# A gated linear-attention kernel: the chunk states computed by an add-then-multiply scan that reads PSUM

## The chip, the cores and the metric

The kernel runs on one core of one Trainium2 chip. The metric is device microseconds of one execution, as the median of several runs. The profile comes from one execution of its own.

## The reference

Three layers follow each other on a batch of 4 sequences of 768 tokens. The first is a gated linear attention with 8 heads of width 48, and it is the one that the change touches:

```
for t in range(S):
    state = alpha[:, :, t, :, None] * state + einsum('bhd,bhe->bhde', k[:, :, t], v[:, :, t])
    y[:, :, t] = einsum('bhd,bhde->bhe', q[:, :, t], state)
```

The second layer mixes each token with the one before it (`mu * x + (1 - mu) * x_prev`, once for keys, once for a gate), then computes `sigmoid(xr @ w_r) * (relu(xk @ w_k)**2 @ w_v)` with widths 384, 1024, 384. The third layer adds a rank-32 product along the sequence (`U`, `V`) and then a two-layer MLP of width 1536 (`w_ch1`, `w_ch2`), and adds its input.

## The kernel before

**Blocks.** The tokens are cut into 8 blocks of 384 (two halves for each of 4 sequences). `moe1(n)` is the second layer of block n, `moe2(n)` the third. All eight `moe1` come first, then all eight `moe2`. Their matrix products are done as three fp32r products of high and low parts (`mm3`), 128x128 by 384 columns each.

**Attention.** `attention(u)` works on a unit: four heads of one block, as two pairs of heads (`ph`, a pair lies on partitions 0:48 and 64:112). There are two units for each block, 16 in all, 8 of them in the first half of a sequence (`half` 0) and 8 in the second (`half` 1), which starts from a state carried over. A block is cut into 3 chunks of 128 tokens. For each pair `prep` forms decay products inside a chunk with two scans on VectorE (`G` backwards, `Fp` forwards; between them a maximum with the least decay on GpSimd, `aC`, and a reciprocal, `bt`) and scales keys and queries. `keys_by_token` transposes the scaled keys of each chunk on TensorE into a PSUM bank (`kk_b`) and ScalarE copies them to `KI`. `scores` forms the masked products within a chunk. `states` multiplies keys and values of each chunk into the same bank `kk_b` (`plan.S48` products), ScalarE copies that to `KV`, a scan over the chunks on VectorE (multiply by the decay `FX`, then add) gives the states at the ends of the chunks (`R`), and two VectorE products with the next chunk's decay give the states at the starts of the chunks (`ST`). In the second half of a sequence four ScalarE products and two VectorE adds first bring in the carried state. `outputs` adds the products of scores with values and of states with queries in two banks, and ScalarE copies them to `Xs`. The fourth pair's 96 rows are then moved by six small DMAs (`spread`) to the rows that the other three leave free.

**Start.** The attention of block 0 comes first (`first_attention`), unit 1, then unit 0. Its query, key and decay loads (`load_qka`) go to three tiles `T`; the pair `ph` 1 reuses the tile of pair 2 and so can be loaded only when that pair has been scaled. Each load of a pair issues one DMA a head. Behind it the weights of `moe1` (`w_k`, `w_v`, `w_r`, stored in 64 bits) are loaded into raw buffers, decoded by ScalarE and VectorE, and split into a high and a low part. DMAs are all issued by SP, in order.

**Order.** The program's instructions are collected as work items with an engine, a cost and dependences. `Plan.schedule` is a list scheduler that puts them in an order for each engine: a first order by due times (`DUE`), then ten rounds by times from a backward pass; the order that ends first in its own model is issued. A PSUM bank counts as one item for dependences. While the planner sees TensorE idle it puts in small bf16 products of a zero tile (L395, `warm`), which write a part of a bank that nobody reads. Where both inputs of a VectorE operation are in SBUF, the planner keeps GpSimd's operations apart from it (`lock`).

**End.** `moe2` adds the last three row tiles to `u` on VectorE into `x2_ring`, a ring of two buffers, and a DMA takes each to the output.

## Time and profile before

| | |
|---|---|
| time, median of 3 runs | 724.15 us (722.25 to 725.62) |
| time of the profiled execution | 724.62 us |
| its span, from the first to the last instruction | 722.9 us |
| TensorE matmul busy | 705.5 us (98%) |
| VectorE busy | 508.5 us (70%) |
| ScalarE busy | 354.5 us (49%) |
| GpSimd busy | 75.8 us (10%) |

The profiled execution took 1.7 us more than its span. TensorE's busy time counts the small products of zeros too. Times within the execution count from the start of the span.

### The profile page before, as it was taken

The numbers are of one execution on the slowest core, as the hardware profiler recorded it, in microseconds if no ns is written. First come the engines' busy times: TensorE is split into PE (matmuls) and PEld (weight loads), VectorE is DVE, ScalarE is ACT, GpSimd is POOL, SyncE is SP. The second block draws the span as 40 slices with busy tenths as digits, with TensorE's granted clock in tenths as the row PEclk, the third lists the DMA queues.
The fourth block names the chain that finished last, engine by engine and source line by source line (L and its number), as shares of the span: only waits on it lengthen the run. The fifth ranks groups of instructions, "written<-read, shape, count | busy, mean of one in ns | idle before, by whom it ended". The sixth has DMA issues, their size and how long they took to land.

```text
span 722.9 us, 13907 instructions
## 1 busy us (share of the span) xinstructions
PE 705.5 (98%) x5319; PEld 675.4 (93%) x5319; DVE 508.5 (70%) x1173; ACT 354.5 (49%) x901; POOL 75.8 (10%) x131
## 2 busy tenths in 40 slices
PE   7999999999999999999999999999999999999995
PEld 7798889899999999999999999999999999999995
DVE  6898987897776567773699999575665657474611
ACT  2588656976767557677797672212121112111210
POOL 2021101442130311311002100000000000000000
PEclk9999989999999999999999999999999999999998
DMA  8835733434333222313253240102020202020001
GB/s 222 200 102 157 186 84 102 108 94 109 85 98 75 63 62 60 98 51 99 65 153 110 66 143 16 51 0 66 1 67 1 65 1 67 1 66 2 34 1 37
DMA packets 29484, 55.46 MB, mean 77 GB/s; under 512 B 5344, under 2 KB 20064, under 8 KB 29408
## 3 DMA queue, kind: packets, MB, share of 16 engines
q1 hardware_dynamic: 29408, 54.48, 27.3%
q8 instruction: 43, 0.70, 0.4%
q14 instruction: 33, 0.27, 0.1%
HBM read 43.85 MB, written 9.44 MB: 74 GB/s over the span
## 4 chain that ended last, share of the span: by engine, by line
PE 74%; DVE 6%; ACT 4%; DMA 3%; issue 1%; SPq 1%; DVEq 0%; ACTq 0%
PE bank L305 73%; DMA arena<-in_qka_dram 3%; ACT arena L320 2%; DVE arena L137 2%; DVE arena L982 2%; DVE rounded L137 1%; PE bank L310 1%; SPq L366 1%; ACT rounded L320 1%; DVE shared L137 1%; ACT shared L320 1%; DMA out_dram<-arena 0%; ACT bank L320 0%; DVE shared L349 0%; DVEq L137 0%
## 5 line engine op out<-in xcount | busy, mean ns | idle before, releaser
L305 PE MATMUL bank<-rounded 128*128 128x384 f32 x2232 | 424.3, 339 | 2.9 <-ACT rounded L320 1.2
L305 PEld LDWEIGHTS bank<-rounded 128*128 128x128 f32 x2232 | 383.7, 186 | 13.2 <-ACT arena L320 2.2
L305 PE MATMUL bank<-rounded,shared 128*128 128x384 f32 x864 | 164.9, 335 | 0.8 <-DVE rounded L137 0.5
L320 ACT ACTIVATE rounded<-bank 128x384 fp32r<-128x384 f32 x160 | 78.3, 489 | 175.4 <-PE bank L305 174.3
L305 PEld LDWEIGHTS bank<-rounded,shared 128*128 128x128 f32 x864 | 150.9, 188 | 1.7 <-DVE rounded L137 1.0
L320 ACT ACTIVATE arena<-arena 128x384 f32<-128x384 f32 (+6 forms) x234 | 103.2, 463 | 48.2 <-DMA arena<-in_qka_dram 29.4
L137 DVE SCALAR_TENSOR_TENSOR rounded<-bank,rounded 128x384 fp32r<-128x384 f32 x96 | 53.4, 556 | 91.4 <-ACT rounded L320 90.3
L982 DVE STREAM_TRANSPOSE arena<-arena 32x96 f32<-32x96 f32 x384 | 103.8, 270 | 5.7
L305 PE MATMUL bank<-shared 128*48 128x128 f32 (+3 forms) x1472 | 100.3, 266 | 3.4 <-DMA shared<-in_v_dram 1.2
L305 PEld LDWEIGHTS bank<-shared 128*48 128x48 f32 (+2 forms) x1472 | 86.6, 142 | 17.8 <-issue 6.2
L320 ACT ACTIVATE rounded<-arena 128x384 fp32r<-128x384 f32 (+2 forms) x137 | 70.4, 522 | 63.6 <-DVE arena L982 49.4
L137 DVE SCALAR_TENSOR_TENSOR arena<-arena 128x384 int32<-128x384 int32 (+2 forms) x140 | 79.9, 590 | 8.9 <-ACT arena L320 8.3
L320 ACT ACTIVATE bank<-bank 128x384 f32<-128x384 f32 x128 | 61.6, 482 | 23.4 <-PE bank L305 22.7
L137 DVE TENSOR_TENSOR rounded<-arena,rounded 128x384 fp32r<-128x384 f32 (+1 forms) x108 | 60.5, 570 | 11.4 <-ACT rounded L320 10.9
L137 DVE TENSOR_TENSOR arena<-bank,arena 128x384 f32<-128x384 f32 (+1 forms) x76 | 41.5, 552 | 25.0 <-PE bank L305 9.9
L137 DVE TENSOR_TENSOR rounded<-bank,rounded 128x384 fp32r<-128x384 f32 x64 | 35.4, 552 | 30.6 <-ACT rounded L320 28.9
L320 ACT ACTIVATE arena<-bank 112x384 f32<-112x384 f32 (+3 forms) x76 | 37.3, 504 | 35.2 <-PE bank L305 33.3
L137 DVE TENSOR_TENSOR shared<-bank,arena 128x384 f32<-128x384 f32 x64 | 33.9, 547 | 24.5 <-PE bank L305 23.0
L137 POOL TENSOR_TENSOR rounded<-arena,rounded 128x384 fp32r<-128x384 f32 (+1 forms) x25 | 27.7, 1116 | 110.5 <-ACT rounded L320 110.4
L395 PE MATMUL bank<-warm 128*128 128x128 bf16 x581 | 37.4, 224 | 1.1 <-DVE arena L543 1.1
L395 PEld LDWEIGHTS <-warm 128*128 128x128 bf16 x581 | 34.5, 101 | 3.1 <-issue 1.5
L349 DVE TENSOR_TENSOR_SCAN shared<-arena 128x384 f32<-128x384 f32 x32 | 31.0, 967 | 4.4 <-ACT arena L320 4.3
(47 smaller groups left out, 258.3 us busy)
## 6 DMA issues: line engine op xcount, KB each, us to landing
arena<-in_qka_dram SPq DMA_DIRECT2D x56, 216.0 KB, 3.7
arena<-in_w_dram SPq DMA_DIRECT2D x24, 384.0 KB, 3.5
shared<-in_v_dram SPq DMA_DIRECT2D x32, 144.0 KB, 3.0
x2d<-arena SPq DMA_DIRECT2D x24, 192.0 KB, 2.2
arena<-x2d SPq DMA_DIRECT2D x8, 576.0 KB, 4.1
out_dram<-arena SPq DMA_DIRECT2D x24, 192.0 KB, 1.9
arena<-in_w_v_dram SPq DMA_DIRECT2D x8, 384.0 KB, 3.2
arena<-in_qka_dram SPq DMA_DIRECT2D x24, 72.0 KB, 2.0
```

What stands on the lines that cost most here:

```text
L137: fn(**args)
L305: "PE", cost, [out], [lhsT, rhs], lambda out, lhsT, rhs: fn(out, lhsT=lhsT, rhs=rhs, start=start, stop=stop),
L310: self.add("PE", cost, [out], [in_, ident], lambda: self.nc.tensor.transpose(out, in_, ident))
L320: self.add("ACT", cost, outs, [in_] + extra, lambda out, in_: fn(out, in_, func, **kw), out=out, in_=in_)
L349: lambda: self.nc.vector.tensor_tensor_scan(out=out, data0=d0, data1=d1, initial=0.0, op0=ALU.mult, op1=ALU.add), True,
L366: lambda: self.nc.sync.dma_start(out, in_),
L395: lambda i: nc.tensor.matmul(banks[SPARE[i]][:, 384:512], lhsT=warm, rhs=warm, start=True, stop=True), FILL_UNTIL, ROUNDS
L982: plan.dve(284, [to], [src], lambda to=to, src=src: nc.vector.transpose(out=to, in_=src))
```

## The change

States: `KV` and the products after the scan go. The bank `kk_b` holds four columns for each head pair and element, and the scan reads it in PSUM: it adds a chunk's sum to the running value, then multiplies by the next chunk's decay, so that its result is already the state at the start of the next chunk. `fc` gets two more columns, a 1 for the first half (the fourth column then resets the scan by a factor 0). ScalarE copies the results to `ST`. In the second half of a sequence the carried state is copied into the bank's first column, and the last chunk's keys are no longer transposed or multiplied with the values, as no state after it is wanted.

Decay floor: the maximum with the least decay moves from GpSimd into the backward scan (`op1=max`, with the floor as the second input).

Start: a fourth tile for `T` lies on two of the raw buffers, so pair 1 has a tile of its own; the weights of `w_k` come in six loads rather than five. Odd heads load 48 rows rather than 64 at the start. The six small DMAs are issued after unit 1, and unit 0 copies its outputs for its two row ranges apart. The planner's cost for a DMA goes from 90 to 56 words a ns.

End: the last adds of `moe2` go into `rs`, three buffers. Operations of `prep` and `check_range` are restricted to partitions 0:112.

```diff
-    mix0_k=468, wk0=-238, wk1=-283, wk2=-17, wk3=45, wk4=60, wkk=7, wv=-12, r0=5, wr=37, early=31, x2=25, u=48, w1=227,
+    mix0_k=468, wk0=-238, wk1=-230, wk2=-220, wk3=38, wk4=45, wk5=60, wkk=7, wv=-12, r0=5, wr=37, early=31, x2=25, u=48, w1=227,
...
-    def scan(self, out, d0, d1):
+    def scan(self, out, d0, d1, op0=ALU.mult, op1=ALU.add):
         self.add(
             "DVE", 66.0 + 2.085 * out.free_size(), [out], [d0, d1],
             lambda: self.nc.vector.tensor_tensor_scan(
-                out=out, data0=d0, data1=d1, initial=0.0, op0=ALU.mult, op1=ALU.add
-            ), True,
+                out=out, data0=d0, data1=d1, initial=0.0, op0=op0, op1=op1
+            ), self.in_sbuf(d0, d1),
         )
...
-            "SP", max(cost, words / 90.0), [out if out_key is None else out_key], [in_ if in_key is None else in_key],
+            "SP", max(cost, words / 56.0), [out if out_key is None else out_key], [in_ if in_key is None else in_key],
...
+    T.append(view(arena, raw_at[2], (KD * TB + 1,)))
...
-    KV = new(2, D, NC)
-    carry = new(2, 2, D)
-    G, Fp, bt = (att(TB) for _ in range(3))
-    aC = new(NC)
+    carry = att(2, 2, D)
+    G, Fp = (att(TB) for _ in range(2))
...
-        nc.vector.memset(ends, 0.0)
+        nc.vector.memset(ends, DECAY_MIN)
...
+    def make_fc():
+
+        nc.gpsimd.memset(fc, 0.0)
+        nc.gpsimd.memset(fc.rearrange("p (b h n) c -> p b h n c", b=B, h=2)[:, :, 0, :, NC], 1.0)
+
+    plan.pool(200, [fc], [], make_fc)
...
-        return T[{2: 0, 3: 1, 0: 2, 1: 0}[ph] if ph < 4 else ph % 3]
+        return T[{2: 0, 3: 1, 0: 2, 1: 3}[ph] if ph < 4 else ph % 3]
...
+                n = D if hh else rows
                 plan.dma(
-                    t[64 * hh : 64 * hh + rows, a * TB : z * TB],
-                    bass.AP(src.tensor, src.offset, [[KD * TB, rows], [1, (z - a) * TB]]), in_key="in", cost=475.0,
+                    t[64 * hh : 64 * hh + n, a * TB : z * TB],
+                    bass.AP(src.tensor, src.offset, [[KD * TB, n], [1, (z - a) * TB]]), in_key="in", cost=475.0,
...
-        plan.act(first, ends[:, 0:NC], AF.Copy)
-        plan.scan(G[:, ::-1], at[:, 1 : TB + 1][:, ::-1], ends[:, ::-1])
-        plan.pool(160, [aC], [g0], lambda: nc.gpsimd.tensor_scalar_max(out=aC, in0=g0, scalar1=DECAY_MIN))
-        plan.dve(110, [bt], [aC], lambda: nc.vector.reciprocal(bt[:, 0:TB:CH], aC))
-        plan.pool(163, [f], [a0, g0], lambda: nc.gpsimd.tensor_tensor(out=f, in0=a0, in1=g0, op=ALU.mult))
+        plan.act(first, ends[BOTH, 0:NC], AF.Copy, scale=0.0)
+        plan.scan(g[:, ::-1], at[:, 1 : TB + 1][:, ::-1], ends[BOTH, ::-1], op1=ALU.max)
+        plan.dve(90, [bt], [g], lambda: nc.vector.reciprocal(bt[BOTH, 0:TB:CH], g[:, 0:TB:CH]))
+        plan.pool(163, [f], [a0, g], lambda: nc.gpsimd.tensor_tensor(out=f, in0=a0, in1=g[:, 0:TB:CH], op=ALU.mult))
         plan.at = due + 6
-        plan.scan(Fp, at[:, 0:TB], bt)
+        plan.scan(fp, at[:, 0:TB], bt[BOTH])
...
         plan.at = due
-        kt, kb = sub(kk_b, NC, 112), KB[ph % 2]
-        for c in range(NC):
+        m = NC - unit(ph // 2)[1]
+        kt, kb = sub(kk_b, m, 112), KB[ph % 2]
+        for c in range(m):
             plan.transpose(kt[:, c, :], kb[BOTH, c * CH : (c + 1) * CH], ident[BOTH, BOTH])
         for h, r in enumerate((EV, OD)):
-            plan.act(KI[ph % 2][:, h], kt[:, :, r], AF.Copy)
+            plan.act(KI[ph % 2][:, h, 0:m], kt[:, :, r], AF.Copy)
 
     def states(u, due):
+
+
 
         half = unit(u)[1]
         plan.at = due
-        kv, vs, st = sub(kk_b, 2, NC, D), VS[u % 2], ST[u % 2]
+        kv, vs, st = sub(kk_b, 2, D, NC + 1), VS[u % 2], ST[u % 2]
+        last = carry[BOTH, u % 2]
+        if half:
+            plan.act(kv[BOTH, :, :, 0], last, AF.Copy)
         for j in range(2):
-            for c in range(NC):
+            for c in range(NC - half):
                 for h, r in enumerate((EV, OD)):
-                    plan.mm(kv[r, j, c, :], KI[j][:, h, c, :], vs[:, h, c, j, :], True, True, plan.S48)
-        f = fc[BOTH, 2 * u : 2 * u + 2, :]
-        last = carry[BOTH, u % 2]
-        plan.act(
-            FX[BOTH, :, :, 1:], f[:, :, 1:].unsqueeze(2).to_broadcast([112, 2, D, NC - 1]), AF.Copy)
-        plan.act(KV[BOTH].rearrange("p j d c -> p j c d"), kv[BOTH], AF.Copy)
-        if half:
-            for j in range(2):
-                for h, r in enumerate((EV, OD)):
-                    plan.act(st[r, h, j, 0, :], carry[r, u % 2, j], AF.Copy, scale=fc[r, 2 * u + j, 0:1])
-            for h, r in enumerate((EV, OD)):
-                plan.tt(KV[r, :, :, 0], KV[r, :, :, 0], st[r, h, :, 0, :], ALU.add)
-        plan.scan(*(t[BOTH].rearrange("p j d c -> p (j d c)") for t in (R, FX, KV)))
+                    plan.mm(kv[r, j, :, half + c], KI[j][:, h, c, :], vs[:, h, c, j, :], True, True, plan.S48)
+        f = fc[BOTH, 2 * u : 2 * u + 2, 1 - half : NC + 2 - half]
+        plan.act(FX[BOTH], f.unsqueeze(2).to_broadcast([112, 2, D, NC + 1]), AF.Copy)
+        plan.scan(*(t[BOTH].rearrange("p j d c -> p (j d c)") for t in (R, kv, FX)), ALU.add, ALU.mult)
         for h, r in enumerate((EV, OD)):
-            plan.tt(
-                st[r, h, :, 1:, :], R[r, :, :, 0 : NC - 1].rearrange("p j d c -> p j c d"),
-                fc[r, 2 * u : 2 * u + 2, 1:].unsqueeze(3).to_broadcast([48, 2, NC - 1, D]), ALU.mult)
+            plan.act(
+                st[r, h, :, 1 - half :, :], R[r, :, :, 0 : NC - 1 + half].rearrange("p j d c -> p j c d"), AF.Copy)
         if not half:
             plan.act(last, R[BOTH, :, :, NC - 1], AF.Copy)
 
-    def outputs(u, due, spread):
+    def outputs(u, due, spread, apart=False):
...
-            plan.act(x[BOTH, p0 + j, 1:], two_b[j][BOTH, 0:TB], AF.Copy)
+            for r in (EV, OD) if apart else (BOTH,):
+                plan.act(x[r, p0 + j, 1:], two_b[j][r, 0:TB], AF.Copy)
...
-            outputs(u, due + 30, i == 1)
+            outputs(u, due + 30, i == 0, i == 1)
...
-            o = x2_ring()
+            o = rs[:, t, :]
...
-        ((P, raw_at[0]), (2 * P, raw_at[1]), (3 * P, rs_at), (P, raw_at[3]), (P, raw_at[0]))
+        ((P, raw_at[0]), (P, raw_at[1]), (3 * P, rs_at), (P, raw_at[2]), (P, raw_at[3]), (P, raw_at[0]))
     ):
-        raw = load_weight(w_k[:, :, c0 : c0 + n], at, -1650 if i < 4 else DUE["wk4"] - 60)
+        raw = load_weight(w_k[:, :, c0 : c0 + n], at, -1650 if i < 3 else DUE[f"wk{i}"] - 60)
```

## Rows read from the trace of the kernel before

**Rows 1.** Windows: stretch, length, busy (x) PE, PEld, DVE, ACT, POOL; clock, DMA, GB/s.
```profile
10.00:20.00 10.00, 7.95 (x119) 6.90 (x118) 6.44 (x11) 3.82 (x14) 0.79 (x3) 1.00 1.06 275
...
40.00:50.00 10.00, 9.43 (x153) 8.93 (x151) 9.30 (x21) 9.41 (x24) 2.18 (x1) 1.00 0.24 81
...
73.30:100.00 26.70, 25.79 (x266) 22.48 (x266) 24.46 (x49) 17.21 (x54) 2.40 (x8) 1.00 0.61 137
100.00:360.00 260.00, 258.85 (x2136) 240.68 (x2135) 184.66 (x349) 176.74 (x484) 54.66 (x86) 0.99 0.31 83
```

**Rows 2.** Windows, instructions of line L395 alone (the products of zeros).
```profile
0.00:73.30 73.30, 37.43 (x581) 34.50 (x581) 1.00 0.65 172
73.30:712.50 639.20, 0.00 (x0) 0.00 (x0) 0.99 0.24 66
```

**Rows 3.** Timeline of TensorE: start, us, operation, xcount, idle before and its releaser.
```profile
86.11 0.74 PE L305 MATMUL bank<-shared 128*48 128x48 f32 x24
86.78 0.44 PE L305 MATMUL bank<-rounded 128*128 128x384 f32 x1
...
88.81 0.51 PE L310 MATMUL bank<-arena,shared 112*128 112x112 f32 x3 [0.39 <-ACT arena L320]
```

**Rows 4.** The chain of work, in order of time: start, us, what.
```profile
154.10 0.29 PE bank L310 x3
```

**Rows 5.** Timeline of the end, TensorE, then VectorE, then SP.
```profile
714.95 0.69 PE L305 MATMUL bank<-shared,rounded 128*128 128x384 f32 x3
...
714.97 0.56 DVE L137 TENSOR_TENSOR arena<-bank,arena 128x384 f32<-128x384 f32 x1 [1.87 <-PE bank L305]
716.72 0.56 DVE L137 TENSOR_TENSOR arena<-bank,arena 128x384 f32<-128x384 f32 x1 [1.19 <-DMA out_dram<-arena]
```

**Rows 6.** Groups of instructions by form, whole span: busy us, mean ns | idle before.
```profile
L349 DVE TENSOR_TENSOR_SCAN shared<-arena,shared 128x384 f32<-128x384 f32 x32 | 31.7, 989 | 0.4
...
L349 DVE TENSOR_TENSOR_SCAN shared<-shared,arena 112x288 f32<-112x288 f32 x16 | 11.9, 747 | 1.1 <-ACT arena L320 1.1
...
L137 DVE TENSOR_TENSOR shared<-shared,arena 48x192 f32<-48x192 f32 x32 | 13.1, 409 | 0.4
...
L137 DVE TENSOR_TENSOR arena<-arena,shared 48x96 f32<-48x96 f32 x16 | 4.5, 279 | 0.3
...
L137 DVE TENSOR_TENSOR shared<-bank,arena 128x384 f32<-128x384 f32 x64 | 33.9, 547 | 24.5 <-PE bank L305 23.0 <-ACT arena L320 1.1
...
L137 DVE TENSOR_TENSOR shared<-arena,shared 128x384 f32<-128x384 f32 x44 | 23.9, 547 | 1.2 <-PE bank L305 0.7 <-DMA arena<-in_qka_dram 0.5
```

**Rows 7.** The same view, ScalarE and GpSimd.
```profile
L320 ACT ACTIVATE arena<-bank 112x288 f32<-112x288 f32 x16 | 9.0, 562 | 11.1 <-PE bank L305 10.7 <-PE bank L395 0.2
...
L320 ACT ACTIVATE shared<-arena 48x48 f32<-48x48 f32 x32 | 10.5, 328 | 0.3
...
L320 ACT ACTIVATE shared<-arena 112x192 f32<-112x192 f32 x16 | 5.7, 359 | 0.1
...
L320 ACT ACTIVATE arena<-shared 112x96 f32<-112x96 f32 x8 | 2.7, 332 | 5.9 <-DVE shared L349 5.7
...
L712 POOL TENSOR_SCALAR arena<-shared 128x3 f32<-128x3 f32 x32 | 12.7, 398 | 125.4 <-DVE shared L349 118.6 <-DVE shared L713 6.7
...
L320 ACT ACTIVATE arena<-bank 112x384 f32<-112x384 f32 x32 | 14.9, 489 | 12.3 <-PE bank L305 12.1
```

**Rows 8.** Timelines of the start: VectorE, then SP.
```profile
17.87 0.96 DVE L349 TENSOR_TENSOR_SCAN shared<-arena 128x384 f32<-128x384 f32 x1 [1.57 <-ACT arena L320]
...
36.72 0.56 DVE L137 TENSOR_TENSOR rounded<-arena,rounded 128x384 fp32r<-128x384 f32 x1 [1.47 <-ACT rounded L320]
...
9.25 1.11 SPq L366 DMA_DIRECT2D arena<-in_qka_dram  x2
...
32.38 0.52 SPq L366 DMA_DIRECT2D arena<-arena  x1
```

**Rows 9.** Windows of all instructions, a stretch at the low clock.
```profile
103.30:110.20 6.90, 6.90 (x48) 6.23 (x49) 4.71 (x9) 2.01 (x6) 0.38 (x2) 0.51 0.37 86
```

More of the change, by code (lines that the diff above doesn't have):

```diff
@@ L447, in fast_path @@
     low = new(NPH)
-    fc = new(NPH, NC)
+    fc = new(NPH, NC + 2)
     firsts = new(NPH, NC)
@@ L490, in fast_path @@
     VS = [att(2, NC, 2, D) for _ in range(2)]
-    FX, R = (att(2, D, NC) for _ in range(2))
+    FX, R = (att(2, D, NC + 1) for _ in range(2))
     ST = [att(2, 2, NC, D) for _ in range(2)]
-    KV = new(2, D, NC)
-    carry = new(2, 2, D)
-    G, Fp, bt = (att(TB) for _ in range(3))
-    aC = new(NC)
+    carry = att(2, 2, D)
+    G, Fp = (att(TB) for _ in range(2))
+    bt = new(TB)
     w1h, w1l = (view(shared, i * KD * DF2, (KD, DF2), F32R) for i in range(2))
@@ L554, in fast_path @@
     plan.dve(400, [bt], [], lambda: nc.vector.memset(bt, 0.0))
+    plan.pool(60, [low], [], lambda: nc.gpsimd.memset(low, 0.0))
+    def make_fc():
+        nc.gpsimd.memset(fc, 0.0)
+        nc.gpsimd.memset(fc.rearrange("p (b h n) c -> p b h n c", b=B, h=2)[:, :, 0, :, NC], 1.0)
+    plan.pool(200, [fc], [], make_fc)
     def make_tri():
@@ L567, in fast_path @@
         plan.pool(600, [t], [], lambda t=t: nc.gpsimd.memset(t, 0.0))
-    plan.pool(130, [FX[:, :, :, 0]], [], lambda: nc.gpsimd.memset(FX[:, :, :, 0], 0.0))
-    for t in banks[5:8]:
-        plan.dve(600, [t[32:64]], [], lambda t=t: nc.vector.memset(t[32:64], 0.0))
+    for t in (banks[5], banks[6][32:64], banks[7][32:64]):
+        plan.dve(600, [t], [], lambda t=t: nc.vector.memset(t, 0.0))
     def next_raw():
@@ L696, in check_pair @@
     def check_pair(ph, t):
-        there = junk[:, 0 : t.free_size()].rearrange("p (c t) -> p c t", c=t.shape[1])
-        plan.act(there, t, AF.Relu, scale=-1.0, bias=ALPHA_MIN, accum_out=low[:, ph : ph + 1])
+        there = junk[BOTH, 0 : t.free_size()].rearrange("p (c t) -> p c t", c=t.shape[1])
+        plan.act(there, t, AF.Relu, scale=-1.0, bias=ALPHA_MIN, accum_out=low[BOTH, ph : ph + 1])
     def prep(ph, due, engs):
-        qt, kt, at = q_k_a(tile_of(ph))
-        g0, f, a0 = G[:, 0:TB:CH], fc[:, ph, :], firsts[:, ph, :]
+        qt, kt, at = (t[BOTH] for t in q_k_a(tile_of(ph)))
+        g, fp, f, a0, first = G[BOTH], Fp[BOTH], fc[BOTH, ph, 0:NC], firsts[BOTH, ph, :], at[:, 0:TB:CH]
         if ph >= CHECK_LATER:
@@ L1029, in check_first @@
         plan.at = due
-        check_pair(ph, q_k_a(T[2])[2][:, 0:TB].unsqueeze(1))
+        check_pair(ph, q_k_a(T[2])[2][BOTH, 0:TB].unsqueeze(1))
     def check_range():
-        one = ck[:, 4:5]
+        c, one = ck[BOTH], ck[:, 4:5]
         for r, x in ((slice(0, P), 0.0), (EV, 1.0), (OD, 1.0)):
             plan.dve(70, [one[r]], [], lambda r=r, x=x: nc.vector.memset(one[r], x))
-        plan.dve(280, [ck[:, 5:6]], [firsts], lambda: nc.vector.tensor_reduce(
-            out=ck[:, 5:6], in_=firsts, axis=AX.XY, op=ALU.min))
-        plan.ts(ck[:, 5:6], ck[:, 5:6], ALPHA_MIN, None, op0=ALU.is_ge)
-        plan.dve(110, [ck[:, 0:1]], [low], lambda: nc.vector.tensor_reduce(
-            out=ck[:, 0:1], in_=low, axis=AX.X, op=ALU.max))
-        plan.dve(280, [ck[:, 1:2]], [fc], lambda: nc.vector.tensor_reduce(
-            out=ck[:, 1:2], in_=fc, axis=AX.XY, op=ALU.max))
-        plan.ts(ck[:, 2:3], ck[:, 0:1], 0.0, None, op0=ALU.is_le)
-        plan.ts(ck[:, 3:4], ck[:, 1:2], DECAY_MAX, None, op0=ALU.is_le)
-        plan.tt(ck[:, 2:3], ck[:, 2:3], ck[:, 3:4], ALU.mult)
-        plan.tt(ck[:, 2:3], ck[:, 2:3], ck[:, 5:6], ALU.mult)
+        plan.dve(280, [c[:, 5:6]], [firsts], lambda: nc.vector.tensor_reduce(
+            out=c[:, 5:6], in_=firsts[BOTH], axis=AX.XY, op=ALU.min))
+        plan.ts(c[:, 5:6], c[:, 5:6], ALPHA_MIN, None, op0=ALU.is_ge)
+        plan.dve(110, [c[:, 0:1]], [low], lambda: nc.vector.tensor_reduce(
+            out=c[:, 0:1], in_=low[BOTH], axis=AX.X, op=ALU.max))
+        plan.dve(280, [c[:, 1:2]], [fc], lambda: nc.vector.tensor_reduce(
+            out=c[:, 1:2], in_=fc[BOTH], axis=AX.XY, op=ALU.max))
+        plan.ts(c[:, 2:3], c[:, 0:1], 0.0, None, op0=ALU.is_le)
+        plan.ts(c[:, 3:4], c[:, 1:2], DECAY_MAX, None, op0=ALU.is_le)
+        plan.tt(c[:, 2:3], c[:, 2:3], c[:, 3:4], ALU.mult)
+        plan.tt(c[:, 2:3], c[:, 2:3], c[:, 5:6], ALU.mult)
         ps = kk_b[0:1, 0:1]
-        plan.mm(ps, ck[:, 2:3], one, True, True, 60.0)
+        plan.mm(ps, c[:, 2:3], one[BOTH], True, True, 60.0)
         plan.dve(70, ["ok"], [ps], lambda: nc.vector.tensor_copy(ok_i, ps))
```

5 lines of the change are left out of this document (2 added, 3 removed).

## The prediction

> **What bounds the kernel now.** I read the windows first, stage by stage, because a share over the whole span mixes two regimes. In the long middle TensorE never rests: busy 258.85 of 260 us between 100 and 360, while VectorE has 184.66 and ScalarE 176.74 [rows 1]. Whatever leaves TensorE's queue there shortens the run one for one, and whatever leaves VectorE or GpSimd is worth nothing there. The start is the other regime. TensorE looks busy too, but the windows of L395 alone say what with: 581 products of zeros, all before 73.3 us [rows 2]. Those are fillers that the planner puts where it sees TensorE without work, so before 73 us the limit is elsewhere. Between 40 and 50 us VectorE is at 9.30 and ScalarE at 9.41 of 10; between 10 and 20 the DMA engines are at 1.06 of their time with 275 GB/s [rows 1]. So the start is first a matter of loads, then of VectorE and ScalarE together, and TensorE can run full only once they have delivered. VectorE stays nearly full up to 100 us (24.46 of 26.7) with TensorE short of work for 26.7 - 25.79 = 0.91 us. The third place is the end: the last product ends at 714.95 + 0.69 = 715.64 us, but the last VectorE add starts only at 716.72, and its releaser is an output DMA [rows 5].
>
> **The middle: TensorE's work.** In the second half of a sequence (8 units, 16 pairs) a third of the transposes goes, 16 in all, and of the key-value products 2 pairs x 2 heads for each unit, 32 in all. A product is fp32 and shows as two instructions: the 12 of a unit stand as x24. They start at 86.11 and the next product starts at 86.78, so one instruction holds the queue for 0.67 / 24 = 28 ns [rows 3]. That is 64 x 28 = 1.79 us. Three transposes take 0.29 us on the chain, 97 ns each [rows 4], so 16 x 97 = 1.55 us. Sum: **3.34 us** less. Nothing hides this gain, because no filler is left after 73.3 us. The products that stay now write every fourth word of the bank; no row shows such a write. Below, it costs nothing; above, I allow a doubling, (192 - 32) x 2 x 28 ns = 9.0 us. I take nothing, because the key-value product's 28 ns are the shortest spacing in the rows and the address step changes no count of columns.
>
> **The middle: VectorE, ScalarE, GpSimd.** In the first half a unit loses a scan of 288 elements (747 ns) and two products (409 ns each) and gets a scan of 384 elements (989 ns): 1.565 to 0.989, 0.58 us less. In the second half two adds of 279 ns go as well: 2.123 to 0.989, 1.13 us less [rows 6]. The scan now reads PSUM. The nearest rows are VectorE products of one size with one input in PSUM or both in SBUF: 547 and 547 ns [rows 6], so I take no surcharge; with 0.1 us for each of the 16 scans VectorE would lose 1.6 of the 13.7 us that it gains. [...]
>
> ScalarE in the first half loses the copy to `KV` (562) and has a copy of 384 in place of 192 elements for `FX` and two copies to `ST` (192 elements each, like the 359 row). Copies of 96, 192 and 384 elements stand at 332, 359 and 489 ns, one of 288 at 562 with a rearranged output [rows 7]; so for 384 elements with a broadcast input I take 0.52, and 0.44 for 288. The sum is 0.36 + 0.56 + 0.33 = 1.25 before and 0.52 + 2 x 0.36 + 0.33 = 1.57 after, 0.32 us more. In the second half the four 328 ns products go: 2.23 before, 0.33 + 0.52 + 2 x 0.44 = 1.73 after, 0.50 us less [rows 7]. In the middle all of this is covered by TensorE, which has more to do than either engine; without that cover ScalarE would gain 8 x (0.50 - 0.32) = 1.4 us. GpSimd loses 32 maxima of 398 ns; it is busy for a tenth of the run, and the step only shortens the way between the two scans of `prep`. I cost it at nothing, as the scans wait in a full VectorE queue.
>
> **The start.** The four units of blocks 0 and 1 run before 100 us. Those of block 0 save 2 x 0.58 = 1.15 us of VectorE where VectorE is the limit; that counts in full. Those of block 1 save 2.27 us, but by then TensorE wants only 0.91 us more [rows 1], so I count 0.9. Pair 1 gets a tile: before, its loads were issued at 9.25 us, when pair 2 had freed its tile, and the scan on them began at 17.87 after VectorE had stood idle for 1.57 us [rows 8]. With its own tile the loads go out beside those of the other pairs, and I count the 1.57 us. The 48 rather than 64 rows take 4 x 16 x 4.6 KB = 0.29 MB from a full queue, 1.1 us at 275 GB/s [rows 1]; this makes the same loads land earlier, so I don't count it twice. The small DMAs: two of the six had to wait for unit 0's copies (the last kind is issued at 32.38), and VectorE then idles 1.47 us at 36.72 behind ScalarE's rounding of the mixed inputs [rows 8]. Now they wait for unit 1 alone; I count 1.47. Against this, ScalarE has 2 x 0.32 more for the states of block 0 and two more copies of 489 ns for unit 0's outputs [rows 7], 1.6 us, in a stage where it is as full as VectorE. Sum: 1.15 + 0.9 + 1.57 + 1.47 - 1.6 = **3.5 us** less. From below nothing, if ScalarE or the weights' loads set the pace; from above 1.15 + 2.27 + 1.57 + 1.47 + 1.1 = 7.6 us, if ScalarE has room. I take the sum, which is near the middle. The six loads of `w_k` rather than five, the new due times and the dearer DMA in the planner's eyes move work about in an order that is made anew; I give that no sign and 2 us in the range either way.
>
> **The end.** With a third buffer the last add follows the last product: 716.72 - 715.64 = **1.08 us** less [rows 5]. From below 0.5, if its DMA then shares the queue with the second. In the seven other blocks the same wait is behind TensorE's back.
>
> **Sum.** 724.62 - 3.34 - 3.5 - 1.08 = 716.7 us for an execution like the profiled one, which is 0.5 us above the median of 724.15.
>
> **Rivals.**
> *The start gives nothing* (ScalarE is as full as VectorE, 9.41 against 9.30 [rows 1]): 724.62 - 3.34 - 1.08 = 720.2 us. For it: the extra 1.6 us of copies. Against: VectorE's idle times are real and behind loads that now come earlier.
> [...]
> *The bank is held* (slower). Before, a copy of 562 ns on ScalarE freed the bank for the next transposes; now the scan on VectorE frees it, 989 ns after it has come to the head of a queue that is 92% full up to 100 us. Even before, transposes at 88.81 stood 0.39 us behind a ScalarE copy into the arena, where `KV` lies too, with every product behind them in TensorE's order [rows 3]. If each unit of blocks 0 and 1 waits 2 us there, 8 us are lost and the start's gain too: 720.2 + 8 = 728.2 us. It decides from 1.9 us a unit over these four, or 0.5 us over all 16. Against it: in the middle VectorE is 71% busy and TensorE has other products to put in between.
> *The order gives it back.* The gain is undone by more changes between long and short products or by DMAs that the dearer price puts later: about 4 us, 724 us, no change.
>
> **Chances.** Forecast (715 to 719 us) 0.50; the start gives nothing 0.15; the low clock goes or the start gives its upper bound 0.17; the order gives it back 0.10; the bank is held, or the write with a step is dear, 0.08. Faster by over 0.5% means under 720.5, slower over 727.8; half a per cent is about what a measurement of this kernel can tell from no change. Of the second case a little over half is under 720.5: 0.50 + 0.17 + 0.08 = 0.75 faster, 0.07 + 0.10 = 0.17 the same, 0.08 slower. The range goes from 711 (the start's upper bound, 712.6, less part of the low clock) to 721.5 (no gain at the start and a little lost to the order); about a tenth lies beyond each end.
>
> **What would show it.** Products on `kk_b`: 64 instructions and 16 transposes fewer, at 28 and 97 ns as before. Fillers that end before 70 us and number under 581. The scan on `kk_b` at about 0.99 us, and no wait of transposes behind it longer than 0.5 us. The first long product before 41 us. The last add within 0.1 us of the last product. I am wrong if the fillers end at 73 us again, if key-value products space out to 50 ns, or if TensorE's idle time after 100 us grows by more than 2 us.

## The result and the profile after

The changed kernel takes **703.92 us** (median of 4 runs, 702.96 to 705.15) against 723.21 us for the kernel before beside it (4 runs), a ratio of 0.973, 95% interval 0.970 to 0.976. The forecast was 716.7 us with a range from 711 to 721.5. The sign was right; the gain is 19.3 us where 7.9 was forecast, so the time lies below the range. The profiled execution took 704.0 us with a span of 702.3 us, 20.6 us shorter than before.

From the page of the changed kernel, busy time, the granted clock and the products of zeros (L395):

```profile
PE 692.5 (99%) x5188; PEld 664.9 (95%) x5188; DVE 491.2 (70%) x1125; ACT 360.2 (51%) x895; POOL 69.7 (10%) x102
...
PEclk9999999999999999999999999999999999999999
...
L395 PE MATMUL bank<-warm 128*128 128x128 bf16 x530 | 35.4, 229 | 1.1 <-DVE arena L543 1.1
```

The windows of the changed kernel, in the stretches of [rows 1], with the same columns:

```profile
10.00:20.00 10.00, 9.75 (x149) 8.49 (x149) 7.87 (x15) 4.14 (x14) 1.32 (x2) 1.00 0.76 179
...
40.00:50.00 10.00, 10.00 (x154) 9.84 (x152) 10.00 (x23) 7.66 (x22) 2.54 (x4) 1.00 0.72 208
...
73.30:100.00 26.70, 26.70 (x284) 22.64 (x278) 23.15 (x45) 18.58 (x55) 1.39 (x4) 1.00 0.57 127
100.00:360.00 260.00, 259.00 (x2078) 242.93 (x2077) 182.78 (x338) 194.27 (x509) 51.30 (x64) 1.00 0.34 91
```

The middle looks as before: TensorE 259.0 of 260 us. The start doesn't. Between 10 and 20 us VectorE does 7.87 us of work where it did 6.44, while the DMA engines move 179 GB/s where they moved 275; between 40 and 50 us they move 208 where it was 81, so transfers now come later. From 73.3 to 100 us TensorE lacks nothing any more. The stretch at a granted clock of 0.51 [rows 9] is gone: the mean granted clock of the profiled execution rose from 0.992 to 0.998.

Now the groups by form that answer to [rows 6, 7], busy us, mean ns and idle before. First three of TensorE in the kernel before, then the changed kernel:

```profile
L305 PE MATMUL bank<-shared 48*128 48x128 f32 x384 | 42.0, 291 | 0.9 <-DVE arena L648 0.9
...
L310 PE MATMUL bank<-arena,shared 112*128 112x112 f32 x96 | 15.6, 267 | 1.9 <-DVE shared L713 1.0 <-ACT shared L320 0.5 <-ACT arena L320 0.4
...
L305 PE MATMUL bank<-shared 128*48 128x48 f32 x384 | 14.6, 211 | 2.1 <-DMA shared<-in_v_dram 1.2 <-ACT shared L320 0.9
```

```profile
L305 PE MATMUL bank<-shared 48*128 48x128 f32 x384 | 40.2, 290 | 0.0
...
L310 PE MATMUL bank<-arena,shared 112*128 112x112 f32 x80 | 13.2, 262 | 0.1
L305 PE MATMUL bank<-shared 128*48 128x48 f32 x320 | 12.9, 212 | 0.2
...
L349 DVE TENSOR_TENSOR_SCAN shared<-arena 112x384 f32<-112x384 f32 x64 | 61.4, 972 | 3.7 <-ACT arena L320 1.9 <-POOL shared L137 1.2 <-issue 0.4
L349 DVE TENSOR_TENSOR_SCAN shared<-bank,shared 112x384 f32<-112x384 f32 x16 | 15.2, 948 | 0.3 <-PE bank L305 0.3
...
L320 ACT ACTIVATE shared<-shared 48x288 f32<-48x288 f32 x16 | 11.5, 721 | 4.4 <-DVE shared L349 4.2
L320 ACT ACTIVATE shared<-shared 48x192 f32<-48x192 f32 x16 | 8.7, 546 | 9.9 <-DVE shared L349 9.7
```

The key-value products are 320 where they were 384, at 212 ns a record where it was 211. Within a run of them one starts 25 ns after another on average (29 ns before), so no cost of writing every fourth word shows here. The transposes are 80 where they were 96, and TensorE waits 0.1 us before them in the whole run, so no wait shows that the bank is held. The scan that reads PSUM takes 948 ns, the same shape from SBUF 972 ns. It is 24 ns cheaper, so the 0.1 us for each of the 16 scans that the prediction sets against a source in PSUM are not there. The copies to `ST` are dear, 546 ns for 192 elements and 721 ns for 288.

The end, timelines of TensorE and of VectorE:

```profile
695.40 0.69 PE L305 MATMUL bank<-shared,rounded 128*128 128x384 f32 x3
...
696.13 0.56 DVE L137 TENSOR_TENSOR arena<-bank,arena 128x384 f32<-128x384 f32 x1 [0.31 <-PE bank L305]
```

The last product ends at 695.40 + 0.69 = 696.09 us and the last add starts 0.04 us later, released by TensorE and no longer by a DMA [rows 5].

**Where the 20.6 us are.** TensorE's records split the span into fillers (L395), idle time and all other work. Idle is the span less the busy time: 17.4 us before, 9.8 after, **7.6 us less**: 6.1 in the first 100 us, 0.4 from 100 to 690, the rest at the end. Fillers: 37.4 before [rows 2], 35.4 after, **2.1 less**. Other work: 668.1 before, 657.1 after, **11.0 less**. The busy times of groups overlap where their records do (those of the changed kernel add up to 770.5 us against 692.5 for TensorE), so they don't add up to this. Counted from the start of each record to the start of the next, less idle time, TensorE has 2.1 us less for the transposes, 2.1 for the key-value products, 1.9 for the products of `scores` (384 each time), 2.8 for the two groups of products in `outputs` and 2.2 for the long products. The low clock, by my estimate 6.9 x (1 - 0.51) = 3.4 us at most, is no term beside these: it lies in the records that ran between 103.3 and 110.2 us [rows 9]. Forecast were 3.5 for the start (idle and fillers there give 8.1), 3.3 for the removed work, 1.1 for the end and nothing for clock, scores and `outputs`.

### The profile page after: what moved, and what is told of

It is laid out like the page before. It is cut to its first block, busy times and chain, and to the rows that moved or that the text cites. A ratio compares the mean times of both kernels' runs of the same rounds, so it can differ in the third digit from the quotient of the medians.

```text
span 702.3 us, 13571 instructions
## 1 busy us (share of the span) xinstructions
PE 692.5 (99%) x5188; PEld 664.9 (95%) x5188; DVE 491.2 (70%) x1125; ACT 360.2 (51%) x895; POOL 69.7 (10%) x102
## 4 chain that ended last, share of the span: by engine, by line
PE 54%; DVE 8%; issue 1%; ACT 0%; DVEq 0%
PE bank L305 54%; DVE rounded L137 3%; DVE arena L987 2%; DVE arena L137 2%; DVE shared L349 1%; DVE shared L137 0%; PE bank L310 0%; ACT bank L320 0%; DVEq L137 0%; DVE arena L720 0%; DVEq L349 0%
## 5 line engine op out<-in xcount | busy, mean ns | idle before, releaser
L320 ACT ACTIVATE arena<-arena 128x384 f32<-128x384 f32 (+5 forms) x234 | 101.7, 462 | 23.0 <-DMA arena<-in_qka_dram 16.2
L320 ACT ACTIVATE rounded<-arena 128x384 fp32r<-128x384 f32 (+3 forms) x137 | 70.4, 523 | 68.0 <-DVE arena L987 48.1
L305 PEld LDWEIGHTS bank<-shared 128*48 128x48 f32 (+2 forms) x1408 | 80.3, 140 | 15.1 <-issue 7.9
L305 PE MATMUL bank<-shared 48*128 48x128 f32 (+3 forms) x1408 | 93.2, 264 | 0.4 <-ACT arena L320 0.2
L320 ACT ACTIVATE bank<-bank 128x384 f32<-128x384 f32 x128 | 61.1, 478 | 18.3 <-PE bank L305 17.4
L349 DVE TENSOR_TENSOR_SCAN shared<-arena 112x384 f32<-112x384 f32 x64 | 61.4, 972 | 3.7 <-ACT arena L320 1.9
L320 ACT ACTIVATE arena<-bank 112x384 f32<-112x384 f32 (+3 forms) x62 | 29.5, 487 | 22.3 <-PE bank L305 20.6
L395 PE MATMUL bank<-warm 128*128 128x128 bf16 x530 | 35.4, 229 | 1.1 <-DVE arena L543 1.1
L395 PEld LDWEIGHTS <-warm 128*128 128x128 bf16 x530 | 32.9, 103 | 2.5 <-DVE arena L543 1.1
```

What stands on the lines that cost most here:

```text
L305: "PE", cost, [out], [lhsT, rhs], lambda out, lhsT, rhs: fn(out, lhsT=lhsT, rhs=rhs, start=start, stop=stop),
L320: self.add("ACT", cost, outs, [in_] + extra, lambda out, in_: fn(out, in_, func, **kw), out=out, in_=in_)
L349: lambda: self.nc.vector.tensor_tensor_scan(out=out, data0=d0, data1=d1, initial=0.0, op0=op0, op1=op1), self.in_sbuf(d0, d1),
L395: lambda i: nc.tensor.matmul(banks[SPARE[i]][:, 384:512], lhsT=warm, rhs=warm, start=True, stop=True), FILL_UNTIL, ROUNDS
```

## The experiments

Orders are made anew by the planner for each kernel, so neighbours differ for no reason of their own: price 58 in place of 56 gives 702.03 us, 1.9 below the changed kernel. I read no single difference under 3 us as the work of an edit without a row for it. The kernel before has medians of 720.8 to 725.2 us beside these experiments; each ratio is to the runs of it that were taken beside that kernel. A useful sum for each kernel is TensorE's **lost time in the first 100 us**, idle plus fillers by the windows; before it is 100 - 92.30 + 37.43 = 45.1 us, after 100 - 98.36 + 35.36 = 37.0. It leaves out what an order loses behind 100 us; where that counts it is said.

### The DMA price alone, and the change without it

```diff
-            "SP", max(cost, words / 90.0), ...
+            "SP", max(cost, words / 56.0), ...
```

> The kernel before with the one edit that the planner prices a DMA at 56 words a ns. Theory A: fillers and idle time up to 75 us shrink by 4 to 7 us, VectorE's wait of 1.5 us at 22 us behind a weight load is gone, time 716 to 720 us. Theory B: 721 to 725 us, as pair 1 still waits for its tile and the mixing for the small DMAs.

> The changed kernel with one edit undone: the planner prices a DMA at 90 words a ns again. Theory A (the price is what shortened the start: with 90 the planner thinks loads land earlier than they do, puts the decoding of weights ahead of attention steps in the queues of VectorE and ScalarE, and both stand behind loads): TensorE's fillers and idle time up to 75 us grow by 4 to 7 us, the first long product moves from 31 us towards 37 or later, time 708 to 711 us. Theory B (the fourth tile and the early small DMAs shortened the start): no more than 2 us, 702 to 706 us, first long product at 31 to 33 us.

The kernel before with this one number changed: **713.39 us** (713.15 to 714.38), ratio 0.987 [0.984, 0.990]. The change with the old number: **715.5 us** (711.54 to 720.1), ratio 0.989 [0.982, 0.995]. Both lie outside what was expected of them, 713.4 below 716 to 720 and 715.5 above 708 to 711: the number that I gave no sign is worth 10 to 12 us, as much as all the rest.

Windows of the first 100 us, in turn of the kernel before, of the kernel before with price 56, of the changed kernel with price 90 (here also its two stretches at a granted clock of 0.50), and of the changed kernel:

```profile
0.00:100.00 100.00, 92.30 (x1151) 83.40 (x1152) 83.97 (x173) 63.35 (x175) 13.49 (x39) 1.00 0.64 163
```

```profile
0.00:100.00 100.00, 98.84 (x1219) 90.05 (x1220) 89.40 (x185) 66.77 (x182) 13.55 (x41) 1.00 0.61 167
```

```profile
0.00:100.00 100.00, 92.77 (x1089) 84.44 (x1089) 83.05 (x166) 67.68 (x178) 9.53 (x31) 0.97 0.63 164
...
15.10:18.50 3.40, 3.40 (x35) 3.18 (x34) 3.40 (x8) 3.13 (x9) 0.76 (x1) 0.50 1.08 368
...
97.00:107.30 10.30, 10.30 (x59) 8.96 (x61) 7.85 (x16) 3.36 (x10) 1.06 (x1) 0.50 0.26 68
```

```profile
0.00:100.00 100.00, 98.36 (x1187) 89.12 (x1187) 86.95 (x174) 70.35 (x188) 11.92 (x32) 1.00 0.67 171
```

With price 90 TensorE is idle for 7 to 8 us of the first 100 in either kernel, with 56 for 1.2 and 1.6. What it waited for at the start stands in the waits of the first 45 us (engine, line, waited for, us in all, times, longest). The kernel before:

```profile
ACT arena L320 <- DMA arena<-in_qka_dram: 11.1, 5, 3.6
DVE shared L349 <- ACT arena L320: 4.4, 4, 1.6
...
ACT arena L320 <- DMA arena<-in_w_k_dram: 2.6, 2, 2.3
```

and with price 56:

```profile
ACT arena L320 <- DMA arena<-in_qka_dram: 7.2, 5, 2.4
...
DVE shared L349 <- ACT arena L320: 1.9, 2, 1.2
```

At price 90 the planner believes that a load of 32-bit words runs at 360 GB/s. The DMA view of the kernel before, first 40 us in slices of 1 us, shows what was moved:

```profile
GB/s 0 0 131 146 303 195 249 230 263 232 223 360 221 218 176 307 354 386 331 179 181 271 301 372 136 25 48 48 251 194 157 333 215 154 136 283 198 316 109 9
DMA packets 4831, 8.24 MB, mean 206 GB/s; under 512 B 735, under 2 KB 3257, under 8 KB 4825
```

The mean of 206 is taken over stretches with loads and without: slices reach 386 GB/s and fall to 9, so it is not the rate of one load. As I read it, the planner at 90 puts ScalarE's and VectorE's work on a load into their queues ahead of its arrival, and work that is ready stands behind it. At 56 words a ns, 224 GB/s, it plans with nearly the mean that it gets, ScalarE's waits behind loads fall from 13.7 to 7.2 us, and no wait behind `w_k` is left. In the changed kernel the same waits are 11.6 us at price 90 and 8.3 at 56. That these waits carry the gain, and not some other difference of the orders, is argued from them and not shown apart.

The rest is clock. The runs of the changed kernel at price 90 took 711.54, 713.5, 717.5 and 720.1 us at mean granted clocks of 0.999, 0.995, 0.990 and 0.987: the two stretches above, 3.4 + 10.3 = 13.7 us at a granted clock of 0.50, are from the profiled execution, the one of 717.5. With no fall the old price still costs 711.5 - 703.9 = 7.6 us. Ahead of the second fall TensorE had waited 1.5 us behind ScalarE, up to 95.59 us. None of the four profiles of the changed kernel with a price from 45 to 72 has a fall before the end. Over all runs of the experiments the mean clock is under 0.995 in 37 of 55 at price 90, the kernel before among them, and in 3 of 64 (the changed kernel's own four included) at 45 to 58. So falls go with the price, but not strictly: the kernel before took 718.9 to 722.0 us in its nine runs at 0.997 or 0.998 and 725.0 to 727.0 in its ten at 0.987 to 0.989. Against the former, price 56 (713.39 us) is worth some 7 us. What in an order brings a fall on is not shown.

### Other prices

```diff
-            "SP", max(cost, words / 56.0), ...
+            "SP", max(cost, words / 58.0), ...   # and 45.0, 72.0
```

> A control: the changed kernel with the planner's price at 58 instead of 56 words a ns, which means nothing for the loads but makes another order. If the order made anew is a lottery of a few us, the time moves by 1 to 4 us either way; if the order is robust near a right price, 702.5 to 705.5 us.

> The changed kernel with the price at 45 words a ns, dearer than the loads are. If the right price is what counts, a slightly too dear one makes the planner wait a little but leaves no queue behind a load: 703 to 708 us. If dearer is always better: under 702 us.

> The changed kernel with the price at 72 words a ns, between 56 and 90. If the time follows how far the price is from what the loads do (206 GB/s in the first 40 us, 51 words of 4 bytes a ns): between 704 and 715.5 us, some 707 to 711 us. If only the particular order at 90 was unlucky: 700 to 706 us.

| price, words a ns | 45 | 56 | 58 | 72 | 90 |
|---|---|---|---|---|---|
| time, us | 706.28 | 703.92 | 702.03 | 708.48 | 715.5 |
| idle, first 100 us | 1.07 | 1.64 | 1.93 | 5.20 | 7.23 |
| idle, 100 to 690 us | 1.29 | 1.96 | 1.68 | 4.04 | 4.82 |

TensorE's idle time grows with a price that promises too fast a transfer, in the middle too, while its fillers in the first 100 us stay between 34.8 and 36.8 us (price 45 has 1.5 us more of them behind 100 us). From 45 to 58 the differences are those of neighbouring orders, so 56 is no sharp optimum.

### Start edits: on their own, and taken back one by one

On the kernel before at price 90: the fourth tile, six loads of `w_k` with the new due times and the small DMAs after unit 1. Then the changed kernel with the tile of pair 1 shared again, with the small DMAs late again, and with all start edits undone (48 rows too) but price 56 kept.

```diff
-        ((P, raw_at[0]), (P, raw_at[1]), (3 * P, rs_at), (P, raw_at[2]), (P, raw_at[3]), (P, raw_at[0]))
+        ((P, raw_at[0]), (2 * P, raw_at[1]), (3 * P, rs_at), (P, raw_at[3]), (P, raw_at[0]))   # new_old_start
...
-        return T[{2: 0, 3: 1, 0: 2, 1: 3}[ph] if ph < 4 else ph % 3]
+        return T[{2: 0, 3: 1, 0: 2, 1: 0}[ph] if ph < 4 else ph % 3]   # new_tile3
...
-            outputs(u, due + 30, i == 0, i == 1)
+            outputs(u, due + 30, i == 1)                                # new_spread_late
```

> The kernel before with the start's edits alone (fourth tile, w_k in six loads, early small DMAs) and the price still at 90. If the price is what counts: the queues still stand behind loads, 719 to 725 us. If the prediction's account of the start holds without the price: 2 to 4 us less, 719 to 721 us; and were the start's edits the cause of all that was not expected, 711 to 715 us.

> The changed kernel with pair 1 back in the tile of pair 2. Theory A (the price): at most 2 us, 703 to 706 us, as pair 1's decay landed only 0.9 us earlier with its own tile (16.46 instead of 17.34 us). Theory B (the tile): pair 1's loads go out some 2 us later again, unit 0 ends 2 to 4 us later, time 706 to 709 us.

> The changed kernel with the six small DMAs issued after unit 0 again, and its outputs copied in one piece. Theory A: under 2 us, 703 to 706 us. Theory B (they stood on the way from unit 0's outputs to the first long product, some 2.5 us from issue to landing): the first long product moves from 31 to 33 or 34 us and the time to 706 to 708 us.

> The changed kernel with all of the start's edits undone (pair 1 in pair 2's tile, small DMAs late, w_k in five loads at the old due times, 64 rows), price 56 kept. If the start's edits count for little at a right price: 700 to 705 us. If they are worth the 3.5 us of the prediction: 706 to 709 us.

Added alone: 724.02 us (10 runs), ratio 0.999 [0.997, 1.002]. Taken back: tile 703.07, ratio 0.972 [0.969, 0.975]; small DMAs 700.67, ratio 0.970 [0.966, 0.973], below what was expected either way; all of them 705.33, ratio 0.976 [0.971, 0.982], between the two expectations, with one of the four runs at 710.85 us and a mean clock of 0.990. The terms of 1.57 and 1.47 us of the forecast are not there in the times of either kernel. The lost time in the first 100 us with all undone is 100 - 98.22 + 35.65 = 37.4 us against 37.0, so the start edits together are worth 0.4 us there.

The small DMAs do what they were meant to do. TensorE's timeline of the changed kernel, then of the one with the small DMAs late:

```profile
30.99 0.62 PE L305 MATMUL bank<-rounded 128*128 128x384 f32 x2 [0.17 <-ACT rounded L320]
...
32.59 14.53 PE L395 MATMUL bank<-warm 128*128 128x128 bf16 x257
...
51.40 9.63 PE L305 MATMUL bank<-rounded 128*128 128x384 f32 x54 [0.15 <-ACT rounded L320]
```

```profile
35.53 0.60 PE L305 MATMUL bank<-rounded 128*128 128x384 f32 x2
...
51.02 9.63 PE L305 MATMUL bank<-rounded 128*128 128x384 f32 x54
```

The first long product comes 4.5 us earlier (in the kernel before it started at 41.01 us). But only 6 of them stand there: 14.5 us of fillers follow, and the long row of 54 starts at 51.40 us against 51.02. Between 40 and 50 us VectorE is busy all of the time (10.00 us), decoding and splitting weights for the most part; as I read it, that is what was late next. The 3.2 us by which late small DMAs are faster are of the size of another thing: the products of `scores` fill 36.9 us there rather than 40.2 (the last experiment says why).

### The states: the scan in PSUM, and the chunk left out

`old_price56_scan` is the kernel before with price 56 and the scan that adds and multiplies in PSUM, with all chunks transposed and multiplied. `new_old_states` is the changed kernel with the old states and the old floor on GpSimd, but the last chunk left out and 64 rows loaded. The other two put the last chunk back or leave it out:

```diff
-        plan.scan(*(t[BOTH].rearrange("p j d c -> p (j d c)") for t in (R, FX, KV)))                     # old_price56_scan;
+        plan.scan(*(t[BOTH].rearrange("p j d c -> p (j d c)") for t in (R, kv, FX)), ALU.add, ALU.mult)   # back in new_old_states
...
-        m = NC - unit(ph // 2)[1]          # new_all_chunks; the reverse, with price 56
+        m = NC                             # and the old states: old_price56_fewer
...
-            for c in range(NC - half):
+            for c in range(NC):
```

> The kernel before with the price at 56 and the states by the scan in PSUM with all chunks, the decay floor on GpSimd, the start and the end as before. If the new states as such are worth what is missing between 710.4 us (all but scan, floor and 48 rows) and 703.9 us: some 6 us under the 713.4 us of the price alone, 706 to 709 us. If it is the order that differs: within 3 us of it, 711 to 716 us.

> Everything of the change but the scan in PSUM (states with the copy to KV, the old scan and the products after it), the decay floor and the 48 rows: price 56, fourth tile, early small DMAs, last chunk left out, third buffer at the end. If the scan itself counts for little because VectorE is not the limit once the order is right: 702 to 706 us, within the 3 us by which one order differs from the next. If VectorE's 13.7 us and the shorter way to the states count in the start: 707 to 710 us.

> The changed kernel with the last chunk's transposes and key-value products done in the second half of a sequence too (their results meet a factor 0). If TensorE's removed work counts one for one, 64 instructions at 28 ns and 16 transposes at 97 ns come back: plus 3.3 us, 706 to 708 us. If what the new order gained hides it: no difference, 703 to 705 us.

> The kernel before with the price at 56 and the last chunk's transposes and products left out in the second half, the states computed as before. If the removed work counts one for one: 3.3 us under the 713.4 us of the price alone, 709 to 711 us. If the rest of the difference to the changed kernel needs the scan in PSUM: the same.

| kernel | us | ratio | lost time, first 100 us |
|---|---|---|---|
| before, price 56 | 713.39 | 0.987 [0.984, 0.990] | 40.4 |
| the same, last chunk left out | 712.79 | 0.985 [0.979, 0.990] | 41.8 |
| changed, old states | 710.39 | 0.981 [0.977, 0.986] | 42.0 |
| before, price 56, scan in PSUM | 709.78 | 0.981 [0.977, 0.984] | 36.6 |
| changed, all chunks | 705.38 | 0.975 [0.970, 0.981] | 38.0 |
| changed | 703.92 | 0.973 [0.970, 0.976] | 37.0 |

The last column falls in two groups: 40.4 to 42.0 us with the old states, 36.6 to 38.0 with the new ones, whatever the start edits. The new states thus take about 4 us of lost time out of the first 100 us. Windows of L395 with price 56, first of the old states, then with the scan in PSUM (TensorE's idle time in the first 100 us, 1.16 and 1.52, hardly differs):

```profile
0.00:50.00 50.00, 33.70 (x520) 1.00 0.69 188
50.00:100.00 50.00, 5.49 (x80) 1.00 0.53 147
```

```profile
0.00:50.00 50.00, 32.98 (x509) 1.00 0.68 186
50.00:100.00 50.00, 2.14 (x29) 1.00 0.67 175
```

The saving is mostly after 50 us: 80 fillers become 29. But not all of it lasts. The next 50 us of the kernel with the scan, all of TensorE and then L395:

```profile
100.00:150.00 50.00, 48.31 (x386) 1.00 0.43 106
```

```profile
100.00:150.00 50.00, 1.29 (x20) 1.00 0.43 106
```

Counted to 150 us the lost time is 36.6 + 1.7 + 1.3 = 39.6 us against 40.7 with price 56 alone: 1.1 us less, not 4. Between `new_old_states` and the changed kernel, which differ in the floor and the 48 rows too, it is 42.9 against 37.1. So what the new states give the start is between 1 and 6 us, by the kernel in which it is read. In time the scan gives 713.39 - 709.78 = 3.6 us on the kernel before, of which 2.1 us are `scores` in a denser order (counted by starts, 38.5 against 36.4); `old_price56_scan` and `new_all_chunks` ended between what the two theories expected, and `new_old_states`, 710.39 us, just above the 707 to 710 of its second.

The chunk left out gives 0.6 and 1.5 us of time by the medians, each within its interval of both nothing and the 3.3 us of the forecast. By the starts of the records it is there, 3.2 us with the old states and 3.3 with the new ones; in the first pair 2.9 us more of idle time and 1.0 of fillers in the whole run eat it up, in the second `scores` take 1.7 us more.

### The floor and the end

```diff
-        plan.scan(g[:, ::-1], at[:, 1 : TB + 1][:, ::-1], ends[BOTH, ::-1], op1=ALU.max)
+        plan.scan(g[:, ::-1], at[:, 1 : TB + 1][:, ::-1], ends[BOTH, ::-1])
+        plan.pool(160, [ac], [g], lambda: nc.gpsimd.tensor_scalar_max(out=ac, in0=g[:, 0:TB:CH], ...))  # new_floor_pool
...
-            o = rs[:, t, :]
+            o = x2_ring()                                                                              # new_ring
```

> The changed kernel with the maximum of the decay floor on GpSimd again, between the backward scan and the reciprocal. If the step on GpSimd cost time in the way between the two scans (0.4 us for each of the four pairs of block 0): 705 to 707 us. If nothing stands behind it, as the prediction has it: 702 to 705 us.

> The changed kernel with the ring of two buffers at the end. The last VectorE add waits for an output DMA again: about 1.1 us between the last product and the last add, which is the working of the prediction; 704 to 706 us. If the order of the rest changes, the end alone, read from the trace, is longer by 1.1 us.

With the maximum on GpSimd again 704.29 us, ratio 0.973 [0.970, 0.977]: the floor in the scan is worth nothing, as costed. With the ring of two again 704.11 us, ratio 0.972 [0.968, 0.976]. The time doesn't tell the two apart, the timelines of its end do (TensorE, then VectorE):

```profile
694.22 0.69 PE L305 MATMUL bank<-shared,rounded 128*128 128x384 f32 x3
...
696.22 0.56 DVE L137 TENSOR_TENSOR arena<-bank,arena 128x384 f32<-128x384 f32 x1 [1.59 <-DMA out_dram<-arena]
```

The add comes 696.22 - 694.91 = 1.31 us after the last product, behind an output DMA, where the changed kernel has 0.04. The end gains what was forecast; its last product came 1.2 us earlier in another order, which is why the medians agree.

### A version that beats both: the scores of two heads in turn

In the timelines of TensorE the 12 instructions of a pair's `scores` products take 1.19 us before (166.24 to 167.43) and 0.87 us after (153.55 to 154.42):

```profile
166.24 1.26 PE L305 MATMUL bank<-shared 48*128 48x128 f32 x12
167.43 2.89 PE L305 MATMUL bank<-rounded 128*128 128x384 f32 x15
```

```profile
153.55 0.94 PE L305 MATMUL bank<-shared 48*128 48x128 f32 x12
154.42 3.42 PE L305 MATMUL bank<-rounded 128*128 128x384 f32 x18
```

Of the 11 steps from one start to the next three are 4 to 6 ns before, the others 106 to 214. After, six are 13 to 15 ns, in turn with steps of 97 to 99 (one of 200). The heads of a pair lie on partitions 0:48 and 64:112; from these starts I took it that their products overlap when they come in turn, and that the planner's order leaves this to chance. The edit makes the two heads' products of a chunk one item, with `SCORE` at 330 for the two rather than 165 for each:

```diff
-            for h, r in enumerate((EV, OD)):
-                plan.mm(sc[h][:, c, :], kb[r, cs], qg[r, cs], True, True, plan.SCORE)
+            two = [(sc[h][:, c, :], kb[r, cs], qg[r, cs]) for h, r in enumerate((EV, OD))]
+            plan.add(
+                "PE", plan.SCORE, [t[0] for t in two], [a for t in two for a in t[1:]],
+                lambda two=two: [plan.nc.tensor.matmul(o, lhsT=l, rhs=x, start=True, stop=True) for o, l, x in two])
```

It ran on the changed kernel with the small DMAs late, on the kernel before with price 56, and on the changed kernel as it is:

> The changed kernel with the small DMAs late again (700.7 us) and the two heads' score products of a chunk kept side by side as one item of the planner. In the traces a pair of heads takes 0.87 us where the two heads alternate (7 and 102 ns apart) and 1.19 us where they don't. If the alternation is what counts, score products take 28 to 30 us in all instead of 34.9, and the time is 694 to 698 us. If the order merely reshuffles: 699 to 703 us.

> The kernel before with the price at 56 and the two heads' score products of a chunk as one item. If the alternation of the heads gives its gain whatever the order: score products' records 30 us in all, and 5 to 9 us under the 713.4 us of the price alone, 704 to 708 us. If the 691.8 us came from a lucky order: 711 to 715 us.

> The changed kernel, small DMAs early as it has them, with the score products of a chunk as one item. If the alternation counts by itself: records 30 instead of 40.2 us, time 692 to 697 us. If it needs the late small DMAs: 700 to 704 us.

They take **691.79 us** (691.35 to 692.51), ratio 0.956 [0.950, 0.962], below the 694 to 698 expected; 702.0 us, 0.972 [0.969, 0.976], below the 704 to 708 expected; and 694.5 us, 0.962 [0.959, 0.966], as expected. The edit alone is worth 703.92 - 694.5 = 9.4 us on the changed kernel, 700.67 - 691.79 = 8.9 with late small DMAs and 713.39 - 702.0 = 11.4 at price 56 without the change. The score products' group of the pair version of the changed kernel:

```profile
L739 PE MATMUL bank<-shared 48*128 48x128 f32 x384 | 30.5, 289 | 0.2 <-ACT arena L320 0.2
```

The same 384 instructions at the same 289 ns each fill 30.5 us of TensorE rather than 40.2: they overlap more. That is 9.7 us for a gain of 9.4. With late small DMAs the group goes from 36.9 to 30.0 us for 8.9, at price 56 without the change from 41.3 to 30.5 for 11.4. And the starts show how: 184 to 192 of the 384 come within 15 ns of the one before in the three pair versions, 105 to 128 in the kernels that they were made from.

## Why the prediction was right in sign and too small

**The step that failed** is in the part on the start: "The six loads of `w_k` rather than five, the new due times and the dearer DMA in the planner's eyes move work about in an order that is made anew; I give that no sign and 2 us in the range either way." The price alone is worth 10 us, some 7 of them without the clock. The rows to size it were there: 206 GB/s moved in the first 40 us on average against the 360 that the old number means, and 13.7 us of ScalarE's waits behind loads. I read the loads as the limit of the start; they were also planned wrong, and this part was free to take.

**Start, 3.5 us.** The lost time of the first 100 us fell by 8.1 us, above the upper bound of 7.6. Price 56 gives about 5 of it (45.1 to 40.4 us on the kernel before; on the changed kernel 100 - 92.77 + 34.77 = 42.0 at price 90 to 37.0), the new states about 4 (40.4 to 36.6), the start edits 0.4; the pieces come from different kernels and need not add up to 8.1. So the terms for the tile (1.57) and the small DMAs (1.47) failed: neither edit alone gains anything that can be measured, though the first long product came 4.5 us earlier by the small DMAs. What was late next, as I read it, was the work behind it, which waits for a full VectorE (10.00 of 10 us between 40 and 50). The term for VectorE's savings (1.15 + 0.9, less 0.64 for ScalarE) had the right mechanism, fewer fillers where VectorE is the limit; by the count to 100 us it was too small by about 2.5, by the counts to 150 us it lies within what the runs give, so its size stays open.

**Low clock.** The lower end of the range takes off "part of the low clock", and no run shows how much that part is. What the traces show is 6.9 us at a granted 0.51 before [rows 9], at most 3.4 us by the estimate above, and a mean of 1.00 from 0 to 690 us in the changed kernel. The fall went, and the runs tie that to the price: old_price56, without any other edit, has a mean clock of 0.996 to 0.998 in its four runs, 3 of 64 runs at a price of 45 to 58 fall under 0.995 and 37 of 55 at 90. Fewer short products are not what it takes: old_price56 has all of them.

**Removed work, 3.34 us.** As forecast by the starts of the records, 3.2 and 3.3 us in the two pairs that differ in nothing else; the runs' times, at 0.6 and 1.5 us, can't resolve it. **PSUM read, stepped write, floor, end:** as forecast, 0, 0, 0 and 1.08 (the last add comes 0.04 us after the last product where it was 1.08). **ScalarE's copies to `ST`** were mis-sized, 0.546 and 0.721 against 0.36 and 0.44: the 359 ns row that stood for them is the copy to `FX`, which repeats a few values, where the copies to `ST` read every fourth word; in the first half ScalarE therefore has about 0.7 us a unit more rather than 0.32, and it is covered all the same. **The bank held** did not come: transposes idle 0.1 us. **The order gives it back** came with the other sign.

Still open: the 2.8 us of `outputs` and 2.2 of long products in the accounting, what the new states alone give the start, how much of the order's 1 to 3 us between neighbours belongs to which edit, and what makes a given order drop the clock.

## What to carry to other kernels

A list scheduler is only as good as its prices: compare the rate that it assumes for transfers with the rate that the trace shows, before any edit of instructions, and treat a changed price as a term with a sign. Where a planner fills idle time, add fillers and idle time into one lost time per stage; either alone hides what a stage lacks. Follow that sum past the stage: what an edit saves in one can be lost in the next. And a gap on an engine is a gain only if what is late next is earlier: two such gaps, filled, gave nothing.

## What was not expected of the hardware

Products of 48 rows on partitions 0:48 and 64:112 overlap more on TensorE when the two alternate: the same 384 instructions fill 30.5 us (new_pairs) rather than 40.2 (the changed kernel). ScalarE's copies that read every fourth word take 546 ns for 192 elements and 721 ns for 288, 1.8 ns for each further element; the copies to `FX`, which repeat a few values, take 359 ns for 192 [rows 7] and 516 ns for 384, 0.8 ns for each further one.
